# A three-stage kernel on one core: GpSimd keeps casts, copies and selects, VectorE takes the subtractions

## The chip, the core and the metric

One core of a Trainium2 chip. The metric is the device time of one execution in microseconds, from which the median of several runs is taken. Five engines work at once, each through its own queue in program order: TensorE (PE; its weight loads are PEld), VectorE (DVE), ScalarE (ACT), GpSimd (POOL) and SyncE (SP), which here issues DMAs. An instruction that waits holds everything behind it on its engine.

## What is computed

A gated linear attention over 4 batches, 8 heads, 768 steps and 48 features, then two feed-forward stages on its 3072 rows of 384 features:

```python
f = 1.0 / (1.0 + np.exp(-f_logit))
for t in range(S):
    state = f[:, :, t, :, None] * state + np.einsum('bhd,bhe->bhde', k[:, :, t], v[:, :, t])
    y[:, :, t] = np.einsum('bhd,bhde->bhe', q[:, :, t], state)
# first stage, d_ff 2048
h = x @ w_in
x = np.where(h >= 1, h, np.where(h <= -1, 0.0, (h + 1) ** 2 / 4)) @ w_out
# second stage, d_ff 1536
g = x @ w_gate
x = (g * sigmoid(g) * (x @ w_val)) @ w_out2
```

The weights arrive as 64-bit floats.

## The kernel before

**Attention** runs in 24 units u (128 steps of one batch, all heads). `at_loadx`, `at_load` and `at_loadv` fetch the gate, q and k, and v. `decay_ops` makes exp and sigmoid of the gate on ScalarE; `at_scan_r` and `at_scan_p` are running products on VectorE (with a small flag instruction behind the first). `at_k` and `at_q` multiply k and q by them; `at_pe1` makes the scores of the unit (`psa`) and transposes k (`pst`), `at_msk` multiplies the scores by a triangle `tri` out of PSUM into `ma` and `mb`, `at_qc` copies part of q beside them. `at_pe2` makes the state's update (`psu`), `at_state` applies it, `at_state_out` copies the state into `vs`, `at_pe3` makes the output `psy`. `at_yc` copies it to `y`, and `at_yd` moves it by six DMAs into the feed-forward input `xl`. Units 0 to 3 make the input of the first pass.

**Feed-forward** runs in 12 passes (`PASSES`): stage 1 for column groups 0 and 1, stage 2 for the same, stage 1 for groups 2 and 3, and so on. A pass takes 512 rows. Every product is made of three matmuls (`mm3`, L375 to L377): operands are split into a rounded half and a rest (high part and low part), and high x high, high x low, low x high are summed. `split_h`/`split_l` split x, `g_hi`/`g_lo` split the activations, where `g_lo` goes to GpSimd for every second activation of the first 32. A stage-1 pass makes 16 tiles: `lin` (`hp`), `h_relu` and `h_sq` on ScalarE, the maximum `h_max` on VectorE (L604), the split, `o_mm` (`acc`).

**Weights** are converted once, in 16 tiles of stage 1 and 18 of stage 2, 128 x 768 each, and the result is stored to DRAM and read back in later passes. Conversion of a tile: load `raw` (`c_dma`), scale the upper words on ScalarE (`c_b`, L332), shift the lower words on VectorE (`c_sh`, L336), an OR and a sign on VectorE (`c_or` L340, `c_sg` L346), the high part on ScalarE (`c_h`, L352), the low part as a subtraction on GpSimd (`c_l`, L356). There are two `raw` buffers; the first seven tiles use slots of the ring `w` (18 slots) in their place.

**The order.** A planner (`Planner`) lays all steps out in time: each step has an engine, an estimated duration, what it depends on, slots that it takes and gives, and a due time (`prio`). Of the steps of an engine that could start within a small window, the one with the earliest due time is written next. What it writes is each engine's fixed order. Into gaps that it sees on TensorE before 60 us it writes filler matmuls (`wt`, L654). `at_base` gives the due times of attention units: units 0 to 3 before the first pass, units 4 to 7 in pass 0, units 8 to 11 in pass 3, and so on.

Of the kernel before, what the change touches and what calls it, by code (L numbers as in the profile page):

```python
# [263 lines left out]
def fast_path(ctx: ExitStack, tc: tile.TileContext, qk, xx, vv, w1, w2, fi, out):  # L264
# [299 lines left out]
    def at_yd(u, X, n):  # L564
# [4 lines left out]
        nc.sync.dma_start(out=xl[0:48, :, sl], in_=yr[0:48, 0:3])  # L569
        nc.sync.dma_start(out=xl[48:96, :, sl], in_=yr[64:112, 0:3])  # L570
        nc.sync.dma_start(out=xl[96:128, 0, sl], in_=yr[0:32, 3])
        nc.sync.dma_start(out=xl[96:112, 1, sl], in_=yr[32:48, 3])
        nc.sync.dma_start(out=xl[112:128, 1, sl], in_=yr[64:80, 3])
        nc.sync.dma_start(out=xl[96:128, 2, sl], in_=yr[80:112, 3])
# [118 lines left out]
    def leave(u, p3):  # L693
# [4 lines left out]
        if odd:  # L698
# [9 lines left out]
            sh = add("ACT", 0.85, lambda n=n, sl=sl: split_h(*getX(n), sl), (yd,), b + 5)  # L708
            E.setdefault(("x", n), []).append(add("DVE", 1.05, lambda n=n, sl=sl: split_l(*getX(n), sl), (sh,), b + 5))

    for u in range(NU):
# [8 lines left out]
        if u == b0:  # L720
# [6 lines left out]
            if u == 0:  # L727
# [4 lines left out]
                ads = [add("DVE", 0.45, lambda i=i, F=F: F[i][2](), (exs[i],), b - 2 + i) for i in range(2)]  # L732
                for i in range(2):
                    E["sg", i], E["ad", i] = sgs[i], ads[i]
            else:
# [4 lines left out]
                ad = add("DVE", 0.75, lambda F=F: F[None][2](), (ex,), b - 2)  # L740
# [238 lines left out]
```

## Time and profile before

| | us |
|---|---|
| median of 3 runs | 991.72 (988.01 to 993.29) |
| profiled execution, its own time | 991.42 |
| span of the profiled execution | 989.4 |
| PE busy | 954.5 (96%) |
| DVE busy | 583.5 (59%) |
| ACT busy | 490.0 (50%) |
| POOL busy | 114.3 (12%) |

The page's shares are means over the whole span. The slices tell the stages apart: DVE is at nine tenths and over for the first quarter and between two and seven tenths in the last three quarters, POOL works in the first quarter only, PE is at nine tenths and over from the tenth slice on. The views that cut the span at the program's own landmarks are shown below.

### The profile page before, as it was taken

What the parts mean: (1) busy time and instruction counts of PE and PEld (TensorE: products, weight loads), DVE (VectorE), ACT (ScalarE), POOL (GpSimd) and SP (SyncE); (2) the same over time, 40 slices, a digit from 0 to 9 for tenths busy, and PEclk for the clock granted to TensorE, in tenths of its full rate; (3) what the DMA queues carried; (4) which work ended last, traced back from release to release, by engine and by line L of the source; (5) the groups of instructions that cost most, each with busy time, mean ns of one, the idle gap of its engine ahead of it and who ended that gap; (6) DMA issues with size and microseconds to landing.
All of it is one profiled execution on the core that took longest, in us unless ns stands there. A gap on an engine that the chain in (4) does not pass through costs nothing.

```text
span 989.4 us, 16323 instructions
## 1 busy us (share of the span) xinstructions
PE 954.5 (96%) x6658; PEld 782.7 (79%) x6658; DVE 583.5 (59%) x840; ACT 490.0 (50%) x772; POOL 114.3 (12%) x78
## 2 busy tenths in 40 slices
PE   8988878999999999999999999999999999999997
PEld 7877656877788888887888888888888888888885
DVE  6899998998763577576633433476544433433332
ACT  5756758775532546578643212356565544222111
POOL 3154444443320000000000000000000000000000
PEclk9999989999999999999999999999999999999999
DMA  9786788678754667322855002667320554200001
GB/s 257 221 278 210 246 260 257 204 219 266 243 191 128 214 215 233 111 54 78 254 193 191 28 1 85 210 227 237 92 59 17 194 193 171 81 1 26 7 1 35
DMA packets 51954, 153.00 MB, mean 155 GB/s; under 512 B 5744, under 2 KB 25712, under 8 KB 51872
## 3 DMA queue, kind: packets, MB, share of 16 engines
q1 hardware_dynamic: 51872, 151.89, 48.5%
q8 instruction: 54, 0.88, 0.4%
q14 instruction: 28, 0.23, 0.1%
HBM read 110.97 MB, written 36.18 MB: 149 GB/s over the span
## 4 chain that ended last, share of the span: by engine, by line
PE 75%; DVE 11%; DMA 6%; issue 3%; ACT 2%; POOL 1%; SPq 1%; DVEq 0%; ACTq 0%; POOLq 0%
PE acc L375 9%; PE acc L376 9%; PE acc L377 9%; PE hp L375 5%; PE hp L376 5%; PE gps L375 5%; PE vps L375 5%; PE hp L377 5%; PE gps L376 5%; PE gps L377 5%; PE vps L377 5%; PE vps L376 5%; DMA raw<-w 4%; DVE raw L340 2%; PE psy L550 2%
## 5 line engine op out<-in xcount | busy, mean ns | idle before, releaser
L376 PE MATMUL acc<-gl,w 128*128 128x512 f32 x504 | 197.1, 391 | 7.6 <-POOL gl L621 5.0
L375 PE MATMUL acc<-gh,w 128*128 128x512 f32 x504 | 197.9, 393 | 0.0
L377 PE MATMUL acc<-gh,w 128*128 128x512 f32 x504 | 196.3, 389 | 0.0
L612 DVE TENSOR_TENSOR sg<-gps,sg 128x512 f32<-128x512 f32 x72 | 49.7, 690 | 126.4 <-ACT sg L608 126.3
L375 PE MATMUL hp<-xh,w 128*128 128x512 f32 x288 | 115.9, 402 | 7.9 <-DVE g L604 6.2
L376 PEld LDWEIGHTS acc<-gl,w 128*128 128x128 f32 x504 | 94.6, 188 | 29.8 <-POOL gl L621 6.4
L376 PE MATMUL hp<-xl,w 128*128 128x512 f32 x288 | 114.0, 396 | 2.1 <-DVE xl L383 2.1
L608 ACT ACTIVATE sg<-gps 128x512 f32<-128x512 f32 x72 | 43.0, 598 | 142.6 <-PE gps L377 130.9
L377 PE MATMUL hp<-xh,w 128*128 128x512 f32 x288 | 113.5, 394 | 0.0
L604 DVE SCALAR_TENSOR_TENSOR g<-g,hp 128x512 f32<-128x512 f32 x96 | 65.3, 683 | 79.9 <-ACT g L601 79.7
L375 PEld LDWEIGHTS acc<-gh,w 128*128 128x128 f32 x504 | 94.6, 188 | 20.2
L377 PEld LDWEIGHTS acc<-gh,w 128*128 128x128 f32 x504 | 94.6, 188 | 19.6
L616 ACT CAST gh<-sg 128x512 fp32r<-128x512 f32 x72 | 44.6, 620 | 112.3 <-DVE sg L612 112.3
L597 ACT ACTIVATE g<-hp,half 128x512 f32<-128x512 f32 x96 | 66.0, 688 | 68.6 <-PE hp L377 64.2
L375 PE MATMUL gps<-xh,w 128*128 128x512 f32 x216 | 85.0, 393 | 0.8 <-DVE sg L612 0.8
L356 POOL TENSOR_TENSOR w<-raw,w 128x768 fp32r<-128x768 f32 x34 | 69.8, 2054 | 138.0 <-ACT w L352 133.9
L616 ACT CAST gh<-g 128x512 fp32r<-128x512 f32 x96 | 59.5, 619 | 52.8 <-DVE g L604 51.1
L375 PE MATMUL vps<-xh,w 128*128 128x512 f32 x216 | 84.5, 391 | 0.0
L376 PE MATMUL gps<-xl,w 128*128 128x512 f32 x216 | 84.1, 389 | 0.0
L377 PE MATMUL gps<-xh,w 128*128 128x512 f32 x216 | 84.1, 389 | 0.0
L377 PE MATMUL vps<-xh,w 128*128 128x512 f32 x216 | 84.1, 389 | 0.0
L376 PE MATMUL vps<-xl,w 128*128 128x512 f32 x216 | 84.0, 389 | 0.0
(94 smaller groups left out, 1553.0 us busy)
## 6 DMA issues: line engine op xcount, KB each, us to landing
w<-w2d SPq DMA_DIRECT2D x36, 768.0 KB, 4.3
raw<-w SPq DMA_DIRECT2D x34, 768.0 KB, 5.9
w<-w1d SPq DMA_DIRECT2D x32, 768.0 KB, 4.6
w2d<-w SPq DMA_DIRECT2D x18, 768.0 KB, 7.4
w1d<-w SPq DMA_DIRECT2D x16, 768.0 KB, 7.2
qk<-qk SPq DMA_DIRECT2D x24, 448.0 KB, 5.3
x<-xx SPq DMA_DIRECT2D x11, 455.0 KB, 6.1
vn<-vv SPq DMA_DIRECT2D x24, 192.0 KB, 5.0
```

Source lines behind the costliest of these rows:

```text
L340: nc.vector.scalar_tensor_tensor(out=lo, in0=hi, scalar=3, in1=lo, op0=ALU.logical_shift_left, op1=ALU.bitwise_or)
L356: nc.gpsimd.tensor_tensor(out=w[:, :, 1, :], in0=jb["t"].rearrange("p (a n) -> p a n", a=2), in1=w[:, :, 0, :].bitcast(F32), op=ALU.subtract,)
L375: nc.tensor.matmul(o, w[:, 0, wsl], xh, start=first, stop=False)
L376: nc.tensor.matmul(o, w[:, 0, wsl], xl, start=False, stop=False)
L377: nc.tensor.matmul(o, w[:, 1, wsl], xh, start=False, stop=last)
L550: nc.tensor.matmul(psy[0:48, i], vs[0:112, 0, c, p], a["ma"][0:112, i], start=True, stop=True)
L597: nc.scalar.activation(g, hp, AF.Relu, bias=half, scale=0.5)
L604: nc.vector.scalar_tensor_tensor(out=g, in0=g, scalar=1.0, in1=hp, op0=ALU.min, op1=ALU.max)
L608: nc.scalar.activation(sg, gps, AF.Sigmoid)
L612: nc.vector.tensor_tensor(out=sg, in0=p, in1=sg, op=ALU.mult)
L616: nc.scalar.copy(gh, g)
```

## The change

Work moves between engines:

- `c_l` (low part of a weight tile) goes from GpSimd to VectorE; `c_h` (its high part, a cast) from ScalarE to GpSimd; `c_sh` of stage 1's tiles from VectorE to ScalarE, where a scale and a rounding of the upper 16 bits do what the shift did.
- all `g_lo` and `at_k` go to VectorE (`POOL_G = 0`, `POOL_K = ()`).
- for units 0 to 7 the mask product of `at_msk` becomes four plain copies on ScalarE (`at_mcopy`) and two selects on GpSimd (`at_msel`).
- `at_qc` and `at_state_out` go from ScalarE to GpSimd.

Order and loads: no step is written more than 35 us before its due time (`HOLD`); the planner's durations are changed; v of units 0 to 3 comes into the same ring slot as q and k; the gate load of unit 2 is due earlier; the last of the first pass's output transfers is split over the SyncE and the ScalarE queue.

```diff
-POOL_K = (0, 1, 2, 3, 4, 5, 6, 7)
-POOL_G = 32
+POOL_K = ()
+POOL_G = 0
+SEL = (0, 1, 2, 3, 4, 5, 6, 7)
+HOLD = 35.0
+PH, SA = (True, True), (True, False)
...
+            t = max(t, o["prio"] - HOLD)
             ready.setdefault(o["eng"], {})[i] = t
...
     def c_sh(jb):
         lo = parts(jb, I32)[0]
-        nc.vector.tensor_scalar(lo, lo, 29, None, op0=ALU.logical_shift_right)
+        if jb["sa"]:
+            top = jb["raw"].bitcast(U16).rearrange("p (n o) -> p n o", o=4)[:, :, 1]
+            nc.scalar.activation(lo, top, AF.Copy, scale=2.0 ** -13, bias=2.0 ** -14 - 0.5)
+        else:
+            nc.vector.tensor_scalar(lo, lo, 29, None, op0=ALU.logical_shift_right)
...
     def c_h(jb):
-        nc.scalar.copy(jb["w"][:, :, 0, :], jb["t"].rearrange("p (a n) -> p a n", a=2))
+        if jb["ph"]:
+            nc.gpsimd.tensor_copy(jb["w"][:, :, 0, :], halves(jb["t"]))
+        else:
+            nc.scalar.copy(jb["w"][:, :, 0, :], halves(jb["t"]))
     def c_l(jb):
-        nc.gpsimd.tensor_tensor(
+        nc.vector.tensor_tensor(
...
     def at_qc(u):
-        nc.scalar.copy(a["mb"][0:64], a["ma"][0:64])
+        nc.gpsimd.tensor_copy(a["mb"][0:64], a["ma"][0:64])
...
+    def at_mcopy(u):
+        for to, of, r in at_scores(u):
+            nc.scalar.copy(to, of)
+    def at_msel(u):
+        for t in (A[u]["ma"][0:64], A[u]["mb"][64:128]):
+            nc.gpsimd.affine_select(
+                out=t, in_=t, pattern=[[0, 8], [1, C]], compare_op=ALU.is_ge, fill=0.0, base=0, channel_multiplier=-1
+            )
...
     def at_state_out(u, c):
-        nc.scalar.copy(vs[64:112, 0, c], ST[b][64:112])
-        nc.scalar.copy(vs[0:48, 1, c], ST[b][0:48])
+        nc.gpsimd.tensor_copy(vs[64:112, 0, c], ST[b][64:112])
+        nc.gpsimd.tensor_copy(vs[0:48, 1, c], ST[b][0:48])
...
+            if u == 3:
+                ys.append(add("ACT", 1.9, lambda u=u, n=n: at_yd(u, getX(n), u % 4 - 1, (None, nc.scalar)), (E["yc", u],), b + 4, (), ("y",), 2.2))
...
-            E["lx", u] = add("SP", 1.6, lambda u=u: at_loadx(u), (), b - 12, ("x",), (), 2.0, (E.get(("l", u - 1)),))
+            E["lx", u] = add("SP", 1.6, lambda u=u: at_loadx(u), (), b - (21 if u == 2 else 12), ("x",), (), 2.0, (E.get(("l", u - 1)) if u != 2 else E["l", 0],))
```

What this does to the orders, at three places. VectorE in pass 0 before, in the middle of a tile's conversion (L336 shift, L340 OR, L346 sign, L604 maximum, L621 low part of g, L447 to L456 scans, L470 product with q):

```order
L336 TENSOR_SCALAR raw<-raw 128x768
L340 SCALAR_TENSOR_TENSOR raw<-raw 128x768
L621 TENSOR_TENSOR gl<-g,gh 128x512
L346 SCALAR_TENSOR_TENSOR raw<-raw 128x768
L604 SCALAR_TENSOR_TENSOR g<-g,hp 128x512
L447 SCALAR_TENSOR_TENSOR e<-e,dr 112x520
L450 SCALAR_TENSOR_TENSOR flag<-e,flag 112x8
L456 SCALAR_TENSOR_TENSOR x<-x,d_118 112x520
L470 TENSOR_TENSOR ma<-qk,x 112x512
```

The same place now (lines of the changed kernel: L374 low part of a weight tile, L482 and L489 products with k and q, L475 scan, L636 maximum, L355 OR, L361 sign, L653 low part of g):

```order
L482 TENSOR_TENSOR qk<-qk,e 112x512
L374 TENSOR_TENSOR w<-raw,w 128x2x384
L475 SCALAR_TENSOR_TENSOR x<-x,d_118 112x520
L489 TENSOR_TENSOR ma<-qk,x 112x512
L636 SCALAR_TENSOR_TENSOR g<-g,hp 128x512
L355 SCALAR_TENSOR_TENSOR raw<-raw 128x768
L653 TENSOR_TENSOR gl<-g,gh 128x512
L361 SCALAR_TENSOR_TENSOR raw<-raw 128x768
```

The shift has left VectorE's queue, and the weight subtraction and the product with k have come into it.

SyncE's loads at the start before, from the second gate on (qk, vn and vs are loads of an attention unit, x a gate, raw a weight tile; qk_305 is unit 2's, qk_446 unit 3's):

```order
L396 DMA x_171<-xx 112x1040
L417 DMA vs1_125<-vv 64x384
L418 DMA vs1_125<-vv 64x384
L324 DMA raw_178<-w1 128x768
L324 DMA raw_272<-w1 128x768
L406 DMA qk_305<-qk 112x1024
L408 DMA vn_307<-vv 128x384
L417 DMA vs0_124<-vv 64x384
L418 DMA vs0_124<-vv 64x384
L324 DMA raw_382<-w1 128x768
L324 DMA raw_394<-w1 128x768
L406 DMA qk_446<-qk 112x1024
```

And now, where qk_160, qk_173 and qk_270 are those of units 1, 2 and 3:

```order
L414 DMA x_158<-xx 112x1040
L426 DMA qk_160<-qk 112x1024
L427 DMA qk_160<-vv 128x384
L436 DMA vs0_124<-vv 64x384
L437 DMA vs0_124<-vv 64x384
L426 DMA qk_173<-qk 112x1024
L427 DMA qk_173<-vv 128x384
L436 DMA vs1_125<-vv 64x384
L437 DMA vs1_125<-vv 64x384
L426 DMA qk_270<-qk 112x1024
L427 DMA qk_270<-vv 128x384
L330 DMA raw_308<-w1 128x768
```

The loads of units 2 and 3 have moved ahead of all weight tiles.

GpSimd around the start of pass 0 before (L356 the weight subtraction, L463 the product with k, L621 the low part of g):

```order
L356 TENSOR_TENSOR w_904<-raw_502,w_904 128x2x384
L463 TENSOR_TENSOR qk_677<-qk_677,e_735 112x512
L621 TENSOR_TENSOR gl_962<-g_918,gh_956 128x512
L356 TENSOR_TENSOR w_1011<-raw_689,w_1011 128x2x384
L621 TENSOR_TENSOR gl_1067<-g_1017,gh_1053 128x512
```

And now (L368 the cast, L493 the copy of q, L537 the selects, L570 and L571 the state copies):

```order
L493 COPY mb_550<-ma_549 64x512
L570 COPY vs1_125<-st3_129 48x192
L571 COPY vs1_125<-st3_129 48x192
L368 CAST w_673<-raw_308 128x2x384
L537 AFFINE_SELECT ma_549<-ma_549 64x512
L537 AFFINE_SELECT mb_550<-mb_550 64x512
L368 CAST w_694<-raw_358 128x2x384
```

Every GpSimd instruction with two inputs is gone; casts stand in one queue with selects and state copies.

## Rows read from the trace of the kernel before

**Rows 1.** The page: busy us, share of the span, instructions.

```profile
PE 954.5 (96%) x6658; PEld 782.7 (79%) x6658; DVE 583.5 (59%) x840; ACT 490.0 (50%) x772; POOL 114.3 (12%) x78
```

**Rows 2.** Stretches: length; PE, PEld, DVE, ACT, POOL busy; PEclk, DMA share, GB/s.

```profile
57.40:63.70 6.30, 6.30 (x30) 4.93 (x31) 6.23 (x5) 3.62 (x5) 4.03 (x2) 0.75 0.98 342
63.70:226.50 162.80, 145.44 (x1025) 114.11 (x1023) 153.44 (x183) 117.71 (x181) 72.25 (x38) 0.98 0.73 235
226.50:309.00 82.50, 81.66 (x361) 67.28 (x360) 55.16 (x72) 35.77 (x50) 19.90 (x10) 1.00 0.62 202
389.90:529.30 139.40, 139.34 (x1019) 113.33 (x1018) 78.32 (x131) 88.95 (x143) 0.00 (x0) 1.00 0.46 144
529.30:982.20 452.90, 452.67 (x2627) 371.46 (x2625) 196.47 (x308) 168.93 (x277) 0.00 (x0) 1.00 0.29 95
```

**Rows 3.** Groups on DVE, 63.7 to 226.5: busy us, mean ns; idle before.

```profile
L340 DVE SCALAR_TENSOR_TENSOR raw<-raw 128x768 int32<-128x768 int32 x20 | 26.0, 1302 | 2.3 <-ACT raw L332 1.6
L346 DVE SCALAR_TENSOR_TENSOR raw<-raw 128x768 int32<-128x768 int32 x20 | 23.5, 1174 | 0.4
...
L336 DVE TENSOR_SCALAR raw<-raw 128x768 int32<-128x768 int32 x20 | 15.2, 762 | 1.0 <-DMA raw<-w 0.9
...
L456 DVE TENSOR_TENSOR_SCAN e<-e,d 112x520 f32<-112x520 f32 x2 | 5.8, 2918 | 0.0
...
L509 DVE TENSOR_TENSOR ma<-psa,tri 64x256 f32<-64x256 f32 x10 | 4.2, 417 | 0.1
```

**Rows 4.** Single lines on DVE: duration ns minimum/median/maximum; first and last start us.

```profile
L340 DVE SCALAR_TENSOR_TENSOR raw<-raw x34: 929/959/2541, 36.8 to 285.3; 128x768 int32<-128x768 int32 x34
...
L336 DVE TENSOR_SCALAR raw<-raw x34: 529/555/1748, 33.6 to 284.2; 128x768 int32<-128x768 int32 x34
...
L456 DVE TENSOR_TENSOR_SCAN x<-x,d x8: 1228/1234/2335, 6.9 to 206.9; 112x520 f32<-112x520 f32 x8
...
L604 DVE SCALAR_TENSOR_TENSOR g<-g,hp x32: 656/678/691, 63.7 to 226.5; 128x512 f32<-128x512 f32 x32
```

**Rows 5.** Single lines on POOL, in the same form.

```profile
L356 POOL TENSOR_TENSOR w<-raw,w x34: 1855/1892/2980, 40.9 to 288.2; 128x768 fp32r<-128x768 f32 x34
...
L621 POOL TENSOR_TENSOR gl<-g,gh x16: 1287/1853/2272, 65.1 to 224.0; 128x512 fp32r<-128x512 f32 x16
```

**Rows 6.** Instructions of DVE in order of time: start us, us.

```profile
55.30 2.03 DVE L383 TENSOR_TENSOR xl<-xl,xh 128x768 fp32r<-128x768 f32 x1 [0.50 <-ACT xh L380]
...
82.97 1.66 DVE L450 SCALAR_TENSOR_TENSOR flag<-e,flag 112x8 f32<-112x8 f32 x1
```

**Rows 7.** Instructions of POOL in order of time, in the same form.

```profile
82.19 2.42 POOL L356 TENSOR_TENSOR w<-raw,w 128x768 fp32r<-128x768 f32 x1 [3.29 <-ACT w L352]
```

**Rows 8.** Groups on POOL over the span: busy us, mean ns; idle before.

```profile
L289 POOL TENSOR_SCALAR_AFFINE_SELECT tri<-tri 64x64 f32<-64x64 f32 x2 | 0.5, 236 | 0.1
masks.py:199 POOL TENSOR_SCALAR_AFFINE_SELECT ident<-ident 128x128 f32<-128x128 f32 x1 | 0.3, 295 | 0.1
```

**Rows 9.** The chain that ended last, 38 to 60 us: start us, us, what.

```profile
39.94 8.55 DMA vs<-vv
...
48.52 5.23 DMA xl<-y
```

**Rows 10.** Waits over the span: us in total, times, longest us.

```profile
POOL w L356 <- ACT w L352: 133.9, 32, 8.4
...
POOL qk L463 <- DMA qk<-qk: 19.8, 3, 10.8
```

**Rows 11.** Instructions of ACT in order of time: start us, us; idle before.

```profile
26.05 0.91 ACT L332 ACTIVATE raw<-raw 128x768 f32<-128x768 f32 x1 [4.25 <-DMA raw<-w]
```

More of the change, by code (lines that the diff above doesn't have):

```diff
@@ L327, in c_dma, with halves @@
             jb["t"] = parts(jb, F32)[0]
+    def halves(t):
+        return t.rearrange("p (a n) -> p a n", a=2)
     def c_b(jb):
@@ L401, in at_load @@
         if u < 4:
-            t = wp.tile([112, 2 * COLS], F32, tag="w", name="qk")
+            r = wp.tile([128, 2 * COLS + DM], F32, tag="w", name="qk")
+            t, vn = r[0:112, 0:2 * COLS], r[:, 2 * COLS:2 * COLS + DM].rearrange("p (h d) -> p h d", h=H)
         else:
             t = ap_.tile([112, 2 * COLS], F32, tag="qk", name="qk")
+            vn = ap_.tile([128, H, D], F32, tag="vn", name="vn")
         nc.sync.dma_start(out=t, in_=qk[u])
-        vn = ap_.tile([128, H, D], F32, tag="vn", name="vn")
         nc.sync.dma_start(out=vn.rearrange("p h d -> p (h d)"), in_=vv[u, :, DM:2 * DM])
@@ L562, in at_yc, with at_yd @@
         nc.scalar.copy(a["y"][64:112, :, u % 2], pv[64:112])
-    def at_yd(u, X, n):
+    def at_yd(u, X, n, engs):
         yr = A[u]["y"].rearrange("p a u t -> p a (u t)")
@@ L568, in at_yd @@
         sl = slice(n * TB, (n + 2) * TB)
[L569 to L574, printed above, removed]
+        pieces = (
+            (slice(0, 48), slice(0, 3), slice(0, 48), slice(0, 3)), (slice(48, 96), slice(0, 3), slice(64, 112), slice(0, 3)),
+            (slice(96, 128), 0, slice(0, 32), 3), (slice(96, 112), 1, slice(32, 48), 3),
+            (slice(112, 128), 1, slice(64, 80), 3), (slice(96, 128), 2, slice(80, 112), 3),
+        )
+        for i, (po, ko, pi, ki) in enumerate(pieces):
+            if engs[i % len(engs)]:
+                engs[i % len(engs)].dma_start(out=xl[po, ko, sl], in_=yr[pi, ki])
     X = {}
@@ L731, in fast_path @@
                 sgs = [add("ACT", 1.9 - 1.28 * i, lambda i=i, F=F: F[i][1](), exs, b - 3 + i) for i in range(2)]
-                ads = [add("DVE", 0.45, lambda i=i, F=F: F[i][2](), (exs[i],), b - 2 + i) for i in range(2)]
+                ads = [add("DVE", 0.4, lambda i=i, F=F: F[i][2](), (exs[i],), b - 2 + i) for i in range(2)]
                 for i in range(2):
@@ L739, in fast_path @@
                     ex, sg = sg, ex
[L740 removed]
+                ad = add("DVE", 0.72, lambda F=F: F[None][2](), (ex,), b - 2)
                 for i in range(2):
@@ L775, in fast_path @@
             todo.append(dict(deps=deps + (E.get(("yc", u - 1)),)))
-    E["fin"] = add("DVE", 0.6, finish, [E["st", u] for u in range(NU)], 1e6)
+    E["fin"] = add("DVE", 0.6, finish, [E["st", u] for u in range(NU)], 800.0)
     last_w = last_d = None
@@ L792, in fast_path @@
                 continue
-            jb = dict(s=s, i=i, run=r, early=s == 1 and i < EARLY)
+            jb = dict(s=s, i=i, run=r, early=s == 1 and i < EARLY, ph=PH[s - 1], sa=SA[s - 1])
             slot = "w" if jb["early"] else "raw"
@@ L798, in fast_path @@
             if wide[s]:
[L799 to L804 removed]
+                cb = add("ACT", 0.93, lambda jb=jb: c_b(jb), (dma,), p)
+                cs = add("ACT" if jb["sa"] else "DVE", 0.92 if jb["sa"] else 0.58, lambda jb=jb: c_sh(jb), (dma,), p)
+                co = add("DVE", 0.97, lambda jb=jb: c_or(jb), (cs, cb), p + 0.1)
+                cg = add("DVE", 0.97, lambda jb=jb: c_sg(jb), (co,), p + 0.2)
+            last_w = ch = add(
+                "Pool" if jb["ph"] else "ACT", 1.05 if jb["ph"] else 0.9, lambda jb=jb: c_h(jb), (cg,), p + 0.1, ("w",),
+                order=(last_w,),
+            )
+            cl = E["w", r, i] = add("DVE", 1.0, lambda jb=jb: c_l(jb), (ch,), p, (), (slot,))
             if again:
```

35 lines of the change are left out of this document (18 added, 17 removed).

## The prediction

> **What bounds the kernel now.** The page's busy shares come first, and they mislead: TensorE is called 96% busy [rows 1], but that mean covers a head with filler matmuls, a stretch where TensorE waits, and a long rest where it never does. So I cut the span by landmarks of the program: the first matmul of pass 0 that has both halves of its input (57.4 us), the first and the 32nd relu maximum on VectorE (63.7 and 226.5, the work of passes 0 and 1), and then the passes after them [rows 2]. From 389.9 to 529.3 the same 32 maxima of passes 4 and 5 take 139.4 us with TensorE busy for 139.34 of them: that pair of passes carries four attention units, as the first pair does, and is bounded by TensorE alone. The first pair takes 162.8 us, and there VectorE is busy 153.44 of them, TensorE 145.44, at a granted clock of 0.98. So VectorE bounds passes 0 and 1, and 162.8 - 139.4 = 23.4 us is the most that freeing it can return there. From 529.3 to 982.2 TensorE is busy 452.67 of 452.9: nothing off TensorE can be won there.
>
> Why VectorE needs 153 us is in the durations. The maximum, which reads one operand from PSUM, takes 656 to 691 ns whatever runs beside it; the OR of the weights, with two operands in SBUF, has a median of 959 and a maximum of 2541 [rows 4]. The long ones lie beside a GpSimd subtraction. A flag instruction over 8 columns that starts at 82.97 ends at 84.63 [rows 6], where the subtraction that began at 82.19 ends at 84.61 [rows 7]. GpSimd and VectorE exclude each other for such instructions. The price, by line (mean in the stretch less the undisturbed duration, times the count [rows 3, 4]): OR 20 x (1.302 - 0.959) = 6.9, sign 20 x (1.174 - 0.959) = 4.3, shift 20 x (0.762 - 0.555) = 4.1, two scans 2 x (2.918 - 1.234) = 3.4, and so on over the nine smaller lines: 36 us in all. GpSimd was busy 72.25 us there [rows 2], so a us of GpSimd costs VectorE 0.50 us. Without it VectorE's work is 153.4 - 36 = 117.4 us, and its idle time 9.4.
>
> **The change, part by part, in the stretch of 162.8 us.** I count what stands between the first and the 32nd maximum in the two orders. VectorE gets 20 weight subtractions (two SBUF operands of 128x768, as the OR: 20 x 0.96 = 19.2), 16 subtractions of g (0.68 each, as the maximum: 10.9), one more OR and sign (1.9). It loses 20 mask products (0.42 [rows 3]: 8.4) and 10 shifts (0.555: 5.6), and the hold moves the attention steps of units 8 to 11 behind the stretch: 4 scans of each kind with their flags (10.5), and 2 products, 4 state steps, 2 additions (4.2). Net +3.3: clean VectorE work 117.4 + 3.3 = 121 us. The change does not lighten VectorE; all depends on the 36 us.
>
> GpSimd's instructions in the stretch are now 20 casts, 8 selects, 4 copies of q and 16 state copies. No row of before has a GpSimd cast, copy or data select, so I bound them. Below: the two selects that built constants take 236 ns for 64 columns and 295 for 128 [rows 8], which is 0.18 + 0.92 ns a column; 768 columns are then 0.885 us, 512 are 0.65, 192 are 0.35, in sum 17.7 + 5.2 + 2.6 + 5.7 = 31 us. Above: the two-input subtraction at its shortest, 1.86 us for 768 columns and 1.29 for 512 [rows 5], with some 0.6 for 192, in sum 63 us. I take 31, since the selects are the only one-input rows that read SBUF. At 0.50 that costs VectorE 15.5 us; if one-input instructions exclude nothing, 0; at 63 us, 31.
>
> The Trainium skill ("SBUF — State Buffer", Who interferes with whom) says that a VectorE instruction with two SBUF inputs contends with any GpSimd instruction that reads SBUF, and not with one that only writes. The maximum and the OR above agree with it on VectorE's side; whether a cast counts as the subtraction did, no run here shows yet. By the rule the price is 15.5 us, without it 0.
>
> So VectorE: 121 + 15.5 + 9.4 idle = 146 us, against TensorE's 139.4. The stretch goes from 162.8 to 146: **-17 us**. ScalarE loses 19 casts, the state copies and the q copies, and gains 9 shifts and 16 score copies in the stretch; 117.71 of 162.8 busy before [rows 2], it stays below 75% of 146 and bounds nothing. Each weight tile of the first stage passes ScalarE twice now (0.91 us each [rows 11]), then VectorE, GpSimd, VectorE; the subtraction that ended it loses about 1 us, so the cycle of the two raw buffers is as long as before.
>
> **The head.** Before, SyncE issues four weight tiles ahead of the last unit's q and k, and GpSimd waits 10.8 us for one such load [rows 10]. Now all four units' loads come first. But the head ends with the last y going to xl, and its chain is a load of vs behind weights (8.55 us) and then the y transfers (5.23) [rows 9]; the same tiles still stand ahead of that transfer, and the transfer is split over two queues. On the other side ScalarE now meets the first weight's multiply before the scores of units 1 to 3; before, it waited there for 4.25 us already [rows 11]. From -7 to +3; I take -3. The split of x at 55.30 took 2.03 us beside a GpSimd subtraction [rows 6]; alone it is as long as the OR of its size, 0.96: -1. From the first full matmul to the first maximum it was 6.3 us at a clock of 0.75 [rows 2], with VectorE's queue in the way; -2 of that.
>
> **Behind the stretch.** From 226.5 to 309 TensorE is busy 81.66 of 82.5 [rows 2]. VectorE gets the rest of the weight subtractions and units 8 to 9 there: 55.16 us before, about 70 now, still under TensorE's time. I cost it at 0 to +4. The q and state copies on GpSimd stand before TensorE's attention steps, with no casts in their queue by then: 0.
>
> **The sum.** -17 - 3 - 1 - 2 = -23 us. The profiled execution took 991.42 us with a span of 989.4; the median of the three runs is 991.72. 991.4 - 23 = **968 us**.
>
> **The rivals.**
> (a) *One-input GpSimd work excludes nothing.* VectorE needs 121 + 9.4 = 130, TensorE bounds the stretch at 139.4, some 141 with the first waits of a queue in order: -22 there, 963 us in sum. For it: no one-input row shows exclusion. Against: the excluded party so far was any VectorE instruction with two SBUF operands, and one with a single operand too (the shift's 0.762).
> (b) *The casts cost what the subtraction cost.* 63 us of GpSimd, VectorE 121 + 31 + 9.4 = 161: the change moves work and wins nothing but part of the head, 988 us.
> (c) *GpSimd's queue becomes the weights' bottleneck, slower.* A cast now stands in one queue with selects, which wait for ScalarE's score copies, which wait for TensorE; and with state copies, which wait for VectorE. While a select waits, the cast behind it waits, and the raw buffer is not freed, so the next weight load is not issued. GpSimd waited for ScalarE 133.9 us in 32 times, 4.2 us a time [rows 10]. If 8 of the 20 casts are held that long and nothing absorbs it, +34 on the stretch's 146: 1002 us. It turns slower than before from 6 held casts on (6 x 4.2 = 25 against 23 won). Against it: seven weight tiles are converted ahead, so only tiles 8 to 16 can stop TensorE.
>
> **How the numbers follow.** Forecast 0.44, (a) 0.33, (b) 0.12, (c) 0.11. About 0.5%, 5 us, is what a measurement of this kernel can tell from no change. (b) lies inside it, (c) beyond it: faster 0.77, same 0.12, slower 0.11. The range takes in (a) with the head's best, 963 - 4 = 959, a little below for a clock that stays full, and the forecast with the head's worst and half of the dearer casts, 968 + 6 + 8 = 982; (b) and (c) are left out. 957 to 983.
>
> **What the profile after would show.** VectorE's OR within some 0.2 us of 0.96 by mean in passes 0 and 1 (a: 0.96; b: 1.3); GpSimd's casts near 0.9 us; 32 maxima in about 146 us, 141 by (a); the first matmul of pass 0 at 52 to 55 us. Wrong would be: casts near 2 us; GpSimd idle before a cast because of a select; TensorE waits behind 309 us; a first matmul later than 58.

## The result

The changed kernel takes **975.1 us** (median of 4 runs, 974.6 to 977.7), the kernel before 991.4 beside it; the ratio is 0.984 (95% interval 0.981 to 0.988). The forecast was 968, its range 957 to 983. The profiled execution took 974.6 us with a span of 972.7.

I cut the span at the landmarks of [rows 2], and also at the 16th and 17th maximum, where pass 0 ends and pass 1 begins. The columns are: start and end, length, busy us of PE, PEld, DVE, ACT and POOL (instructions), granted clock, DMA share, GB/s. First the kernel before, with the stretch of [rows 2] in its three parts:

```profile
63.70:151.30 87.60, 75.25 (x665) 58.58 (x663) 81.69 (x103) 59.39 (x97) 40.21 (x22) 0.96 0.72 235
151.30:162.60 11.30, 9.14 (x38) 6.40 (x36) 11.06 (x13) 10.29 (x15) 2.52 (x2) 1.00 0.78 273
162.60:226.50 63.90, 61.06 (x324) 49.13 (x325) 60.69 (x68) 48.03 (x71) 29.53 (x15) 1.00 0.75 227
```

The changed kernel, the same parts, the stretch as a whole, and passes 4 and 5:

```profile
60.10:138.00 77.90, 72.68 (x656) 56.61 (x654) 71.45 (x97) 58.33 (x95) 31.66 (x34) 1.00 0.75 258
138.00:150.20 12.20, 8.85 (x35) 6.36 (x35) 8.60 (x13) 5.97 (x9) 0.88 (x1) 1.00 0.79 250
150.20:207.70 57.50, 56.80 (x250) 47.03 (x251) 47.07 (x64) 36.12 (x54) 8.59 (x9) 1.00 0.68 218
60.10:207.70 147.60, 138.33 (x941) 110.00 (x940) 127.12 (x170) 100.42 (x157) 41.13 (x44) 1.00 0.72 242
...
373.80:510.70 136.90, 136.73 (x949) 111.37 (x948) 63.71 (x107) 70.85 (x111) 7.23 (x16) 1.00 0.39 128
```

The first maximum comes 3.6 us earlier (63.7 to 60.1), the stretch is 15.2 us shorter (162.8 to 147.6), and from the 32nd maximum to the end it takes 2.1 us longer (762.9 to 765.0): 16.7 us between the two spans. Of the stretch, pass 0 gave 9.7 us and pass 1 6.4, and the time between them grew by 0.9. The granted clock of pass 0 went from 0.96 to 1.00, and TensorE's busy time in it from 75.25 to 72.68 us. Pass 1 is now at TensorE's own time: 57.50 us, of which it works 56.80. It nearly was before (61.06 of 63.90); TensorE works 4.3 us less there now, most of it the scores, transposes and update of one attention unit, which run later. In pass 0 VectorE is busy for 71.45 of 77.90 us and TensorE for 72.68; of the 4.8 us that TensorE is seen to wait there, 3.4 are for VectorE.

The groups on VectorE in the stretch (busy us, mean ns; idle before), which answer to [rows 3]:

```profile
L653 DVE TENSOR_TENSOR gl<-g,gh 128x512 fp32r<-128x512 f32 x31 | 21.6, 699 | 3.1 <-ACT gh L648 3.0
...
L355 DVE SCALAR_TENSOR_TENSOR raw<-raw 128x768 int32<-128x768 int32 x21 | 20.5, 974 | 3.2 <-ACT raw L349 2.3 <-ACT raw L341 0.5
L361 DVE SCALAR_TENSOR_TENSOR raw<-raw 128x768 int32<-128x768 int32 x21 | 20.4, 971 | 0.3
L374 DVE TENSOR_TENSOR w<-raw,w 128x768 fp32r<-128x768 f32 x20 | 20.2, 1011 | 2.9 <-POOL w L368 2.9
```

And GpSimd's, from 60 to 215 us, in the same form:

```profile
L368 POOL CAST w<-raw 128x768 fp32r<-128x768 f32 x22 | 21.9, 996 | 97.5 <-DVE raw L361 94.6 <-issue 2.8
L537 POOL TENSOR_SCALAR_AFFINE_SELECT mb<-mb 64x512 f32<-64x512 f32 x4 | 5.1, 1266 | 0.3
L570 POOL COPY vs<-st 48x192 f32<-48x192 f32 x6 | 4.7, 790 | 2.2 <-DVE st L566 2.0
...
L493 POOL COPY mb<-ma 64x512 f32<-64x512 f32 x3 | 2.5, 831 | 8.0 <-DVE ma L489 8.0
```

The OR fell from a mean of 1302 ns to 974 and the sign from 1174 to 971. The whole surplus of VectorE (for each instruction that lies beside a GpSimd instruction, its time less the median of its like without one) fell from 36 us to 6.0. GpSimd's own instructions are now the stretched ones: the state copy takes 790 ns by mean and 342 undisturbed, the select 1266 and 650. By the undisturbed times (last section) GpSimd's 44 instructions in the stretch would take 29.6 us, and they are busy for 41.1: of the overlap GpSimd now bears some 12 us, VectorE 6.0. And the cast waits for VectorE's sign (94.6 of 97.5 us of idle time), not for a select.

### The profile page after: what moved, and what is told of

Read it like the earlier page. It is cut to its first block, busy times and chain, and to the rows that moved or that the text cites. A ratio compares the mean times of both kernels' runs of the same rounds, so it can differ in the third digit from the quotient of the medians.

```text
span 972.7 us, 16295 instructions
## 1 busy us (share of the span) xinstructions
PE 947.5 (97%) x6606; PEld 778.7 (80%) x6606; DVE 575.0 (59%) x850; ACT 447.3 (46%) x676; POOL 127.6 (13%) x182
## 4 chain that ended last, share of the span: by engine, by line
PE 90%; ACT 2%; DMA 2%; DVE 2%; POOL 1%; issue 1%; SPq 0%; ACTq 0%; POOLq 0%
PE acc L393 11%; PE acc L394 11%; PE acc L395 11%; PE hp L393 6%; PE hp L395 6%; PE hp L394 6%; PE gps L393 5%; PE vps L393 5%; PE gps L394 5%; PE gps L395 5%; PE vps L394 5%; PE vps L395 5%; PE wt L686 3%; DMA raw<-w 2%; PE psy L580 2%; PE pst L510 1%
## 5 line engine op out<-in xcount | busy, mean ns | idle before, releaser
L636 DVE SCALAR_TENSOR_TENSOR g<-g,hp 128x512 f32<-128x512 f32 x96 | 65.5, 685 | 101.0 <-ACT g L633 100.8
L394 PEld LDWEIGHTS acc<-gl,w 128*128 128x128 f32 x504 | 94.6, 188 | 23.0 <-DVE gl L653 3.6
L393 PEld LDWEIGHTS acc<-gh,w 128*128 128x128 f32 x504 | 94.6, 188 | 20.4 <-issue 0.5
L395 PEld LDWEIGHTS acc<-gh,w 128*128 128x128 f32 x504 | 94.6, 188 | 19.5
L653 DVE TENSOR_TENSOR gl<-g,gh 128x512 fp32r<-128x512 f32 x96 | 66.5, 694 | 42.5 <-ACT gh L648 42.1
L648 ACT CAST gh<-g 128x512 fp32r<-128x512 f32 x96 | 59.5, 619 | 60.0 <-DVE g L636 56.1
```

What stands on the lines that cost most here:

```text
L393: nc.tensor.matmul(o, w[:, 0, wsl], xh, start=first, stop=False)
L394: nc.tensor.matmul(o, w[:, 0, wsl], xl, start=False, stop=False)
L395: nc.tensor.matmul(o, w[:, 1, wsl], xh, start=False, stop=last)
L636: nc.vector.scalar_tensor_tensor(out=g, in0=g, scalar=1.0, in1=hp, op0=ALU.min, op1=ALU.max)
L648: nc.scalar.copy(gh, g)
L653: (nc.gpsimd if pool else nc.vector).tensor_tensor(out=gl, in0=g, in1=gh.bitcast(F32), op=ALU.subtract)
```

## What the experiments were to tell apart

The theory after this reading: (1) a two-input subtraction on GpSimd holds VectorE up, a one-input cast, copy or select hardly does, and is held up itself; (2) pass 0 is still bound by VectorE's queue, pass 1 by TensorE; (3) what the head wins is lost again in pass 0. The rivals: the gain came from where the work stands, with no exclusion; GpSimd's idle time is free; the two raw buffers bound pass 0; or the head is worth what it wins.

One table for all runs. The times in a row are from the run's trace: start of the first `hp` matmul, of the 1st, 16th and 32nd maximum; VectorE busy and its surplus (as above) between the 1st and the 32nd.

| kernel | median us | first matmul | 1st | 16th | 32nd | VectorE busy | surplus |
|---|---|---|---|---|---|---|---|
| before | 991.4 | 55.3 | 63.7 | 151.3 | 226.5 | 153.4 | 36.0 |
| changed | 975.1 | 56.3 | 60.1 | 138.0 | 207.7 | 127.1 | 6.0 |
| cl_pool | 990.5 | 58.2 | 67.3 | 149.2 | 221.6 | 125.4 | 25.9 |
| x_sub | 996.5 | 60.0 | 67.3 | 157.9 | 229.1 | 134.3 | 12.9 |
| x_copy | 985.1 | 59.9 | 65.2 | 148.1 | 217.9 | 129.0 | 7.5 |
| raws | 982.5 | 57.5 | 61.3 | 138.6 | 214.7 | 129.9 | 6.7 |
| ph_act | 974.4 | 50.8 | 55.6 | 137.3 | 205.5 | 129.6 | 3.2 |
| sel_none | 993.4 | 54.4 | 59.5 | 150.9 | 221.6 | 137.9 | 4.6 |
| sa_dve | 987.3 | 53.3 | 58.5 | 146.9 | 214.6 | 137.1 | 8.2 |
| no_hold | 980.6 | 57.0 | 60.7 | 140.5 | 214.7 | 136.3 | 6.8 |
| sel_no3 | 978.8 | 50.4 | 56.1 | 139.4 | 210.4 | 129.7 | 6.1 |
| head_act | 980.8 | 50.9 | 56.8 | 141.6 | 212.5 | 132.1 | 5.7 |
| head_frz | 977.6 | 54.5 | 61.0 | 139.7 | 209.9 | 127.5 | 6.2 |
| msk_frz | 977.3 | 52.3 | 57.6 | 140.3 | 210.2 | 132.0 | 4.1 |

A warning on reading it: an edit that changes a step's engine or duration makes the planner write a new order for every queue. Only x_sub, x_copy, head_frz and msk_frz keep the order of the changed kernel.

## Experiments on the exclusion

**cl_pool.** One part undone: the weight tile's subtraction on GpSimd again.

```diff
     def c_l(jb):
-        nc.vector.tensor_tensor(
+        nc.gpsimd.tensor_tensor(
...
-            cl = E["w", r, i] = add("DVE", 1.0, lambda jb=jb: c_l(jb), (ch,), p, (), (slot,))
+            cl = E["w", r, i] = add("Pool", 2.5, lambda jb=jb: c_l(jb), (ch,), p, (), (slot,))
```

> The changed kernel with one part undone: the weight tile's subtraction (its low part) is on GpSimd again, the cast stays there too. Between the first and the 32nd maximum VectorE loses 21 x 0.95 = 20 us of its own work, GpSimd gains 21 x 1.9 = 40 us. Theory (GpSimd's two-input work holds VectorE up, about 0.5 us a us): VectorE's busy time stays near 127 us because the OR's mean goes back to 1.2 to 1.3 us, each raw buffer is held some 1 to 2 us longer a turn, and the time is 978 to 985 us. Rival (the gain came from where the work was put, nothing interacts): VectorE is freed by 20 us, OR's mean stays at 0.97, the time is 968 to 975.

Measured: 990.5 us (ratio to before 1.000, interval 0.999 to 1.002): the whole gain is gone, 5 us more than the theory's upper end. Its stretch, and VectorE's low part of g and sign in it:

```profile
67.30:221.60 154.30, 142.44 (x905) 112.42 (x905) 125.36 (x146) 99.35 (x155) 87.02 (x66) 0.97 0.67 222
```

```profile
L653 DVE TENSOR_TENSOR gl<-g,gh 128x512 fp32r<-128x512 f32 x31 | 30.6, 986 | 5.9 <-ACT gh L648 5.7
L361 DVE SCALAR_TENSOR_TENSOR raw<-raw 128x768 int32<-128x768 int32 x20 | 22.8, 1139 | 0.4
```

VectorE has 24 instructions fewer, among them 20 subtractions that took 20.2 us, and is busy for 125.36 us against 127.12: what left its queue came back as a surplus of 25.9 us against 6.0. The low part of g went from 699 to 986 ns by mean. The OR did not do what I had written for it (997 ns by mean, not 1200 to 1300): in this order other instructions lie beside the subtraction. One of them, on VectorE (start us, us), and the GpSimd subtraction beside it:

```profile
109.54 2.31 DVE L653 TENSOR_TENSOR gl<-g,gh 128x512 fp32r<-128x512 f32 x1
```

```profile
109.09 2.21 POOL L374 TENSOR_TENSOR w<-raw,w 128x768 fp32r<-128x768 f32 x1
```

The surplus rules the rival out: the work was taken from VectorE, and about as much came back in longer instructions. How many of the 15 us belong to the new order, this run does not tell.

**x_sub and x_copy.** The changed kernel with useless work on GpSimd behind each first-stage cast, in a buffer that nobody reads; the first with a two-input, the second with a one-input instruction.

```diff
             nc.gpsimd.tensor_copy(jb["w"][:, :, 0, :], halves(jb["t"]))
+            if jb["s"] == 1:
+                for _ in range(4):
+                    nc.gpsimd.tensor_tensor(out=pad, in0=pad, in1=pad, op=ALU.subtract)
```

In x_copy the last line is this one:

```diff
+                    nc.gpsimd.tensor_copy(pad, pad)
```

> The changed kernel, and behind each cast of a first-stage tile GpSimd makes four useless two-input subtractions of 128x192 in a buffer of its own that nobody reads; about 0.6 us each, 16 x 4 x 0.6 = 38 us in all. GpSimd has some 100 us idle between the first and the 32nd maximum, and waited for VectorE there. Theory (two-input work on GpSimd excludes VectorE): VectorE loses about half of it, 19 us, most of it in the first pass, where weight tiles are late: 983 to 995 us. Rival (idle time of GpSimd is free): 974 to 977 us.

> The same as the run with useless subtractions, but with four useless one-input copies of 128x192: about 0.35 us each, 22 us in all. If one-input work on GpSimd costs VectorE what the forecast took (0.50 us a us): 11 us more on VectorE, 980 to 986 us. If it costs what the stretch of the changed kernel shows (6.0 us of VectorE for 42.1 us of GpSimd, 0.14): 3 us more, 975 to 979. If it costs nothing: 974 to 976.

Measured: 996.5 us (ratio to before 1.006, 1.004 to 1.009) and 985.1 (0.994, 0.992 to 0.997). The useless instructions by line (duration ns minimum/median/maximum; first and last start us), x_sub and then x_copy:

```profile
L373 POOL TENSOR_TENSOR pad<-pad x64: 496/844/3978, 39.4 to 156.9; 128x192 f32<-128x192 f32 x64
```

```profile
L373 POOL COPY pad<-pad x64: 339/688/3975, 40.1 to 147.3; 128x192 f32<-128x192 f32 x64
```

Both are slow because they are held up themselves: a copy that needs 0.34 us took up to 3.98. In x_copy the 11 copies with no two-input VectorE instruction beside them took 0.35 us each, the 53 others 0.94 by mean. VectorE lost 1.5 us to the copies (surplus 7.5 against 6.0, for 35.2 us more of GpSimd: 0.04 a us) and 6.9 us to the subtractions (for 41.0 more: 0.17 a us). So the useless one-input instructions do not cost VectorE the forecast's 0.50, and less than the mix of the changed kernel (6.0 for 41.1: 0.15; the expectations say 0.14, from a sum of single times). Yet the copies cost 10 us in all, the number that I had given to the 0.50. GpSimd's queue shows where, here a stretch of it in x_copy (start us, us; idle before):

```profile
61.72 4.17 POOL L373 COPY pad<-pad 128x192 f32<-128x192 f32 x4
65.84 2.85 POOL L498 COPY mb<-ma 64x512 f32<-64x512 f32 x1
68.64 0.87 POOL L370 CAST w<-raw 128x768 fp32r<-128x768 f32 x1
69.46 3.24 POOL L373 COPY pad<-pad 128x192 f32<-128x192 f32 x4
```

Four copies that need 1.4 us take 4.17, the copy of q behind them takes 2.85 in place of 0.61, and the next cast stands behind both. The cast of the fifth tile begins at 60.19 us (54.19 in the changed kernel), that of the sixteenth at 143.62 (133.51). Half of the 10 us is lost ahead of the first maximum, the other half in pass 0 (82.9 us against 77.9), where VectorE is busy 1.8 us more and idle 3.2 us more. GpSimd had 106 us idle in the stretch of the changed kernel (147.60 less 41.13), and that time was not free. So 985.1 us, which my expectation had put down to the price of 0.50 on VectorE, has another cause; the surplus, not the time, tells the theories apart. For x_sub the time lies 1.5 us above the theory's range (983 to 995, measured 996.5), but VectorE lost 6.9 us, not 19. Of the 21 us, 7.2 were lost ahead of the first maximum, and in the stretch, where the granted clock was 0.96, VectorE's idle time rose by 7.0 us as well: there too much of the loss is not VectorE's surplus.

## Experiments on what bounds pass 0

**raws.** Three more tiles are loaded into ring slots, so that the two raw buffers don't hold up their loads.

```diff
-            jb = dict(s=s, i=i, run=r, early=s == 1 and i < EARLY, ph=PH[s - 1], sa=SA[s - 1])
+            jb = dict(s=s, i=i, run=r, early=s == 1 and (i < EARLY or i in (8, 10, 12)), ph=PH[s - 1], sa=SA[s - 1])
```

> The changed kernel, but tiles 8, 10 and 12 are loaded into slots of the ring too, as the first seven are, so that the two raw buffers no longer bound how early tiles 8 to 13 are loaded. If the cycle of the two raw buffers (load 5.6 us, two passes on ScalarE, OR, sign, cast, low part) bounds the first two passes, the tiles of the first pass come 3 to 8 us earlier, the 32 maxima take 141 to 144 us instead of 147.6, and the time is 967 to 972 us. Rival (VectorE's own work and its queue in order bound it, 127 us busy): the tiles come no earlier by more than 2 us, 974 to 976 us.

Measured: 982.5 us (0.992, 0.990 to 0.995), 7 us slower than the changed kernel, which neither theory had. ScalarE's scaling of tiles 9 and 10 came 12 us earlier (75.78 and 79.53 us; 87.29 and 91.33 in the changed kernel), but VectorE's last step of the two tiles did not. On VectorE of raws, and then of the changed kernel:

```profile
92.63 0.94 DVE L374 TENSOR_TENSOR w<-raw,w 128x768 fp32r<-128x768 f32 x1
...
97.34 0.95 DVE L374 TENSOR_TENSOR w<-raw,w 128x768 fp32r<-128x768 f32 x1
```

```profile
93.35 0.94 DVE L374 TENSOR_TENSOR w<-raw,w 128x768 fp32r<-128x768 f32 x1
...
97.27 0.95 DVE L374 TENSOR_TENSOR w<-raw,w 128x768 fp32r<-128x768 f32 x1
```

So the buffers are not the bound there: VectorE's queue is. The 16th maximum came at 138.6 against 138.0; the time was lost behind it, from there to the 32nd (76.1 us against 69.7), in the new order: 3.9 us between the passes, at a granted clock of 0.79, and 2.5 in pass 1, all of which TensorE works. Which of the order's steps costs them I have not traced.

**ph_act, sel_none, sa_dve, no_hold.** Each undoes one other part: all casts on ScalarE; all masks as products on VectorE; the shift on VectorE; no hold.

```diff
-PH, SA = (True, True), (True, False)
+PH, SA = (False, False), (True, False)     # ph_act
+PH, SA = (True, True), (False, False)      # sa_dve
...
-SEL = (0, 1, 2, 3, 4, 5, 6, 7)
+SEL = ()                                   # sel_none
...
-HOLD = 35.0
+HOLD = 1e9                                 # no_hold
```

> The changed kernel with the weight tiles' cast (the high part) back on ScalarE, for both stages; the subtraction stays on VectorE. GpSimd loses 21 us of its 42 between the first and the 32nd maximum. If a cast on GpSimd takes 0.50 us a us from VectorE, as the forecast had it, VectorE is freed of 10 us there: 963 to 970 us. If one-input work takes next to nothing from VectorE (x_copy: 1.5 us more excess for 36 us more of GpSimd), nothing is won that way, and ScalarE's queue, which loses 0.83 us a tile to it, decides: 972 to 980 us.

> The changed kernel with all masks as products on VectorE (16 x 0.42 = 6.7 us more between the first and the 32nd maximum), no score copies on ScalarE and no selects on GpSimd. Theory (VectorE's order and length still count there, though it is idle for 19.4 us): 3 to 7 us slower behind the first matmul, the head 2 to 4 us faster by the select that no longer waits: 973 to 980 us. Rival (selects cost through GpSimd's queue as much as they free): no loss behind the head, 969 to 972 us.

> The changed kernel with the shift of the first stage's tiles back on VectorE: 8 to 10 x 0.56 us = 4.5 to 5.6 us more on VectorE between the first and the 32nd maximum, 0.8 to 0.9 us a tile less on ScalarE. If VectorE's own length bounds the stretch, the time rises by 4 to 9 us: 979 to 984. If VectorE's 19.4 us of idle time take it up: 973 to 977. If the tile's way through ScalarE twice was what bounds, it is faster: 969 to 973.

> The changed kernel without the rule that holds a step until 35 us before it is due. Unit 8's matmuls (2.4 us of TensorE) and its scans, flags and products (some 8 to 14 us of VectorE) go back ahead of the 32nd maximum. If the hold only moves them (TensorE's 2.4 us come back behind the stretch, where it is full; VectorE had 19.4 us idle): 973 to 977 us, with the 32 maxima taking 2 to 5 us longer and as much won between the 24th gate product of the second stage and the 33rd maximum. If VectorE's queue in order is tight there: 979 to 986 us.

Measured: ph_act 974.4 (0.983, 0.979 to 0.986), the same as the changed kernel; sel_none 993.4 (1.002, 1.000 to 1.004); sa_dve 987.3 (0.996, 0.993 to 0.998); no_hold 980.6 (0.989, 0.986 to 0.992). sel_none and sa_dve lie 13 and 3 us above the highest times that I had written for them.

Without casts GpSimd is busy 21.6 us in place of 41.1, VectorE's surplus falls by 2.8 us (0.14 a us), and the end is the same: with a new order beside it, the casts' move to GpSimd is worth nothing and costs nothing. The three that put work back into VectorE's queue lose 5.5 to 18 us, and most of sel_none's and sa_dve's loss is there by the 16th maximum (12.9 and 8.9 us). Their pass 0, sel_none first (columns as above):

```profile
59.50:150.90 91.40, 77.30 (x664) 58.59 (x664) 81.86 (x122) 54.31 (x80) 24.99 (x28) 0.94 0.67 234
```

```profile
58.50:146.90 88.40, 76.42 (x665) 58.94 (x664) 81.44 (x112) 50.42 (x86) 32.15 (x35) 0.94 0.70 245
```

VectorE is busy for some 90% of pass 0 in each, as in the changed kernel (92%): what is put in lengthens the pass by as much or more (10.4 us busy for 13.5, and 10.0 for 10.5). Not all of that is the part itself: the 16 masks take 6.7 us (0.42 each), the 12 shifts in sa_dve's pass 6.7 (0.56 each), and the new orders bring other work. The granted clock is 0.94 as well, and TensorE works for 77.30 and 76.42 us in place of 72.68; what that adds to the pass was not separated. In no_hold VectorE's busy time in the stretch rises by 9.2 us and the 32nd maximum comes 7.0 later; 0.8 us of that come back behind it (764.2 us to the end, against 765.0). Of the 7.0, 4.2 are in pass 1, where TensorE has one unit's scores and transposes again:

```profile
153.00:214.70 61.70, 59.54 (x292) 48.95 (x293) 53.00 (x72) 42.08 (x60) 13.81 (x11) 1.00 0.81 256
```

**msk_frz.** sel_none lost far more than the 6.7 us that its masks take in the stretch. So the masks once more, in the order that the changed kernel was planned in:

```diff
-            mc = add("ACT", 1.5, lambda u=u: at_mcopy(u), (pa, qc), b + 2.4, (), ("at",) * 2 if u >= 4 else ())
-            mask = add("Pool", 2.3, lambda u=u: at_msel(u), (mc,), b + 2.5)
+            mc = add("ACT", 1.5, lambda u=u: at_msk(u), (pa, qc), b + 2.4, (), ("at",) * 2 if u >= 4 else ())
+            mask = add("Pool", 2.3, lambda: None, (mc,), b + 2.5)
```

> The changed kernel in the order that it was planned in, but for units 0 to 7 the mask is a product on VectorE at the place of ScalarE's score copies, and GpSimd's selects are gone; nothing is planned anew. With the masks on VectorE and a new plan the time was 993.4, 18 us more. If VectorE's length alone counts (16 x 0.42 = 6.7 us between the first and the 32nd maximum): 979 to 984 us. If most of the 18 us came from the new plan: 974 to 978. If the products, which wait for TensorE's scores with VectorE's whole queue behind them, are what costs: 986 to 994, with VectorE idle over 22 us in the stretch.

Measured: 977.3 us (0.986, 0.982 to 0.990), 2.2 over the changed kernel. Its pass 0:

```profile
57.60:140.30 82.70, 74.31 (x654) 57.84 (x653) 76.12 (x114) 52.60 (x79) 24.36 (x27) 0.98 0.75 260
```

From the first to the 16th maximum VectorE is busy 4.7 us more and takes 4.8 us longer, and it began 2.5 us earlier, without the late select. The same masks on VectorE cost 2 us in one order and 18 in the other. So 16 of sel_none's 18 us came from the order that its planner wrote, and the runs that plan anew (cl_pool too) measure a part and an order together. That the subtraction holds VectorE up is shown by the surplus in cl_pool, not by its 15 us.

## Experiments on the head

The first matmul came at 56.3 us, and the first with both halves of its input, the prediction's landmark, at 56.65; before they came at 55.3 and 57.4, and I had 52 to 55. GpSimd, VectorE and TensorE of the changed kernel there (start us, us; idle before, and what ended it):

```profile
38.79 0.65 POOL L537 TENSOR_SCALAR_AFFINE_SELECT ma<-ma 64x512 f32<-64x512 f32 x1
39.51 4.13 POOL L537 TENSOR_SCALAR_AFFINE_SELECT mb<-mb 64x512 f32<-64x512 f32 x1
43.71 1.73 POOL L368 CAST w<-raw 128x768 fp32r<-128x768 f32 x2
```

```profile
38.42 1.23 DVE L566 TENSOR_TENSOR st<-st,e 112x192 f32<-112x192 f32 x1
39.57 0.95 DVE L374 TENSOR_TENSOR w<-raw,w 128x768 fp32r<-128x768 f32 x1
40.44 0.94 DVE L361 SCALAR_TENSOR_TENSOR raw<-raw 128x768 int32<-128x768 int32 x1
41.31 0.94 DVE L401 TENSOR_TENSOR xl<-xl,xh 128x768 fp32r<-128x768 f32 x1
42.18 0.94 DVE L355 SCALAR_TENSOR_TENSOR raw<-raw 128x768 int32<-128x768 int32 x1
```

```profile
43.70 0.26 PE L581 MATMUL psy<-mb,vs 128*48 128x64 f32 x1 [3.04 <-POOL mb L537]
...
44.79 11.60 PE L686 MATMUL wt<-tri 128*64 128x64 f32 x173
56.32 0.50 PE L393 MATMUL hp<-xh,w 128*128 128x512 f32 x1
56.65 0.40 PE L394 MATMUL hp<-xl,w 128*128 128x512 f32 x1
```

The last unit's second select, 0.65 us long, begins while VectorE is in a two-input instruction (L566) with four more right behind it, and ends 0.5 us after the last. It goes the other way too: that first instruction takes 1.23 us, where its line has 0.36 undisturbed, beside GpSimd's cast and first select. TensorE waits 3.0 us for the second select, the last `psy` and `y` are late by that, and the 173 filler matmuls behind `psy` run until 56.3. By then x has been waiting: ScalarE finished its high part at 53.55 us, VectorE its low part at 54.99. No run leaves the fillers out.

**sel_no3, head_act, head_frz.** Unit 3's mask on VectorE; the first five casts on ScalarE, planned anew; the same with the order kept.

```diff
-SEL = (0, 1, 2, 3, 4, 5, 6, 7)
+SEL = (0, 1, 2, 4, 5, 6, 7)     # sel_no3
...
-            jb = dict(s=s, i=i, run=r, early=s == 1 and i < EARLY, ph=PH[s - 1], sa=SA[s - 1])
+            jb = dict(s=s, i=i, run=r, early=s == 1 and i < EARLY, ph=s == 2 or i >= 5, sa=SA[s - 1])     # head_act
...
     def c_h(jb):
-        if jb["ph"]:
+        if jb["ph"] and (jb["s"] == 2 or jb["i"] >= 5):     # head_frz
```

> The changed kernel, but the mask of unit 3, the last before the first pass, is a product on VectorE again. In the changed kernel one of that unit's two selects took 4.14 us on GpSimd in place of 0.65, TensorE waited 3.0 us for it, and the last y and so the first matmul of the first pass (56.4 us) came after it. If the select is what makes the head late, the first matmul comes at 52 to 54.5 us and the time is 970 to 973 us. If the transfers of y or the filler matmuls written ahead of the first matmul hold it anyway: 55.5 to 57, and 974 to 976 us.

> The changed kernel, but the casts of the first five weight tiles, which are converted ahead of the first matmul, are on ScalarE again; all later casts stay on GpSimd. With all casts on ScalarE the first matmul of the first pass came at 51.8 us in place of 56.4, and the stretch of 32 maxima took 149.9 in place of 147.6. If GpSimd's queue in the head (casts between the selects and copies of units 2 and 3) made the head late, the first matmul comes at 51.5 to 53.5, the stretch stays at 147 to 149, and the time is 969 to 972.5 us, better than either. If an earlier start only makes TensorE wait for the weights later (the weight tiles bound the first pass from the start of the span): the stretch takes 150 to 152 and the time is 974 to 977.

> The changed kernel with every queue's order kept as it is, except that the first five tiles' casts are issued on ScalarE at the place in the program where GpSimd had them (the planner is not told, so nothing is planned anew: VectorE, TensorE and SyncE have the same rows in the same order). If casts in GpSimd's queue made the head late, the unit 3 selects no longer stand behind them, the first matmul comes at 52 to 54.5 us, the 32 maxima take 147 to 149 us and the time is 970 to 973.5. If the early first matmul of the run with all casts on ScalarE came from the new order there, nothing is won: first matmul 55.5 to 57, 974 to 977. If ScalarE, which now waits for VectorE's sign ahead of each cast, holds the score and y copies: first matmul 58 to 60, 977 to 980.

Measured: 978.8 (0.988, 0.985 to 0.991), 980.8 (0.989, 0.987 to 0.992) and 977.6 us (0.986, 0.982 to 0.990): none is faster, though the first matmul came at 50.4, 50.9 and 54.5, and sel_no3 and head_act lie above every time that I had written for them. Without unit 3's select, and in a new order, 5.9 us are won at the first matmul. But the 16th maximum comes at 139.4, 141.6 and 139.7 against 138.0. ph_act has the same: 5.5 us earlier at the first matmul, 4.5 at the first maximum, 0.7 at the 16th. VectorE was busy for 17.4 of the 20.1 us ahead of the first maximum in the changed kernel and for 92% of the pass behind it. TensorE can start earlier, but the weights and maxima that it needs in pass 0 come when VectorE's queue gets to them. In head_frz the first matmul came 1.8 us earlier and the first maximum 0.9 later.

## The prediction, step by step

**The stretch, -17 us: right by size (15.2), wrong in its parts, so the size is luck.** VectorE's clean work was put at 121 us, the surplus at 15.5 and the idle time at 9.4. Measured: 127.1 busy with 6.0 of surplus, so 121 of clean work, and some 20 us idle. The mis-sized terms are the price of 0.50 us a us of GpSimd (measured 0.15 over the stretch, 6.0 for 41.1, and 0.04 for the copies of x_copy) and the idle time that I carried over from before; GpSimd's 31 us, right as undisturbed times (29.6), became 41. The errors cancel to 2 us. The idle time failed because I took the stretch as one bound, though in pass 1 TensorE was busy for 61.06 of 63.90 us before, as much as VectorE: VectorE is idle for 6.5 us of pass 0 (5.9 before), but for 10.4 of pass 1, where TensorE is now the bound, and for 3.6 between the passes (0.2 before). There pass 1 waits for its x and then for a raw tile that VectorE's queue has ahead of the maximum:

```profile
143.15 0.83 ACT L398 CAST xh<-xl 128x768 fp32r<-128x768 f32 x1 [0.24 <-DMA xl<-y]
```

```profile
147.28 0.56 DVE L351 TENSOR_SCALAR raw<-raw 128x768 int32<-128x768 int32 x1 [1.43 <-DMA raw<-w]
...
150.16 0.68 DVE L636 SCALAR_TENSOR_TENSOR g<-g,hp 128x512 f32<-128x512 f32 x1
```

From the 16th to the 17th maximum it takes 12.2 us; in passes 4 and 5 that takes 8.2 (444.9 to 453.1). This is the first place to look for more. The floor was off too: the passes 4 and 5 that gave 139.4 carried five units' scores (160 matmuls), not four; with four (128) they take 136.90.

**GpSimd's casts near 0.9 us: right.** Undisturbed 0.88, by mean 1.0, so the estimate from two short selects held. The OR within 0.2 of 0.96: right (0.97).

**Who excludes whom.** The select that ends behind the run of VectorE instructions, and copies that triple, show that a one-input GpSimd instruction that reads SBUF and a two-input VectorE instruction do exclude each other. That agrees with the rule cited ahead (the Trainium skill, "SBUF — State Buffer", Who interferes with whom). The same page of the Trainium skill (SBUF: two separate sides) has the one that starts first hold the shared pair of ports for its whole instruction; here a run of VectorE instructions kept the select out from one to the next. My step from "excludes" to "costs VectorE 0.50" was the error: the excluded party was mostly GpSimd (some 12 us in the stretch, VectorE 6.0).

**The head, -3: wrong; the split and the first maximum, -1 and -2: right, and larger.** The first matmul came 1.0 us later. From it to the first with both halves it took 2.1 us before and 0.3 now, from there to the first maximum 6.3 and 3.4 (granted clock 0.75 and 1.00): 4.6 us in place of 3. So the first maximum came 3.6 earlier, not 6. What failed in the head: its working weighed the loads and ScalarE's queue, and not GpSimd's selects, which stand in the head's chain now and wait for VectorE, nor the fillers behind them. The term was also misplaced: the runs on the head show that up to 5.9 us there return 0.7 at most by the 16th maximum.

**Behind the stretch, 0 to +4, taken as 0: 2.1 us.** From the 32nd to the 33rd maximum it takes 2.7 us longer, from there on 0.6 less (599.5 to 598.9). In the stretch before, unit 8 had its share of attention matmuls; now they run where TensorE has no gaps. The update `psu` in the stretch and from there to the 33rd maximum, before and then changed (columns PE, PEld, DVE busy):

```profile
63.70:226.50 162.80, 3.47 (x160) 2.85 (x160) 3.50 (x10) 0.98 0.73 235
226.50:389.90 163.40, 2.02 (x96) 1.65 (x96) 2.09 (x6) 1.00 0.67 214
```

```profile
60.10:207.70 147.60, 2.99 (x128) 2.38 (x128) 2.81 (x8) 1.00 0.72 242
207.70:373.80 166.10, 2.70 (x128) 2.21 (x128) 2.77 (x8) 1.00 0.67 224
```

32 of 160 matmuls of the update moved out of the stretch, and the scores and transposes of the unit with them. The scores and transposes are the hold's: in no_hold they are back in the stretch (160 and 20 matmuls; 128 and 16 in the changed kernel), and the 33rd maximum comes 163.8 us behind the 32nd, 2.3 less. The update is not back there (128), so that its move is not the hold's alone. The hold was still worth its place: without it the kernel is 5.5 us slower.

**The sum.** -23 forecast, -16.3 by the medians: 2 us short in the stretch, 2 in the head, 2 behind it.

**The rivals.** (a) had the mechanism nearly right on VectorE's side but not its end: TensorE bounds pass 1, not pass 0. (b) did not happen on GpSimd, but cl_pool is what it describes, with the subtraction, and gives before's time. (c) did not happen as written, with casts held behind selects that wait for others; x_copy shows that GpSimd's queue can become the bottleneck, and that some 22 us of copies (64, 0.34 each undisturbed) are enough for 10 us.

**What stays open.** How much of the 16.3 us belongs to each part: the parts that were undone with a new plan sum to more than the gain (15 + 18 + 12 + 5.5). How much of the losses is the granted clock's, and what the fillers cost in the head. Why the 128x768 subtraction costs VectorE 0.43 us a us (cl_pool: 19.9 more of surplus for 45.9 more of GpSimd) and the 128x192 one 0.17. No version ran faster than the changed kernel beyond the spread; ph_act equals it.

## What to carry to other kernels

Ask of a move to GpSimd two questions, not one: how many inputs its instruction has, and who holds on when both engines want the same time. Here a two-input instruction cost the neighbour more than a one-input instruction of its size (0.17 against 0.04 us a us at 128x192, 0.43 for the subtraction of 128x768 against 0.14 for the cast, these two from newly planned runs), and the size counted as much. Either kind also cost its own queue, and whatever waits for that queue. In a kernel whose order is planned from estimated durations, an ablation measures a part and a new order: keep the order fixed (swap the instruction, not the plan) before a number is given to a part.
